# A linear-attention kernel: weight loads alternate, folds run in quarters, outputs and preparations move between slots

## The chip, the cores and the metric

The kernel runs on one core of one Trainium2 chip. The metric is the device time of one execution in microseconds (us), and the figure quoted for a kernel is the median of its runs. A run counts as slow when it is over 1.5% above the fastest of its kernel; unless the text says otherwise the runs below are all fast, and ratios use fast runs alone. A profile is one such execution under the hardware profiler; its span is 1.75 to 1.96 us shorter than the time of the same run (runs of e1 to e12 and of the kernel before beside them), so spans are compared with spans and times with times.

Engines: PE multiplies matrices, PEld loads PE's weights, DVE is the vector engine, ACT the scalar engine, POOL is GpSimd, SP issues the stores.

## The reference

```python
# q, k, v: [8 batches, 8 heads, 576, 64] float32; w_in [512, 2048], w_out [2048, 512]
q_p, k_p = phi(q), phi(k)                 # relu(.) times cos and sin of the position: 128 features
kv  = einsum('bhsf,bhsd->bhfd', k_p, v)
z   = sum(k_p, axis=2)
x   = (q_p @ kv) / (q_p @ z + 1e-6)       # then tokens x 512: x is [4608, 512]
out = softplus(x @ w_in) @ w_out          # [4608, 512] float32
```

The kernel does not run the second half as written. Near zero softplus(h) is close to h/2 + ln 2, so it folds the two weights once into `W_c` = 0.5 · w_in · w_out and a bias, and one product per tile is left. It keeps the squared norm of every row of x and of the weights; at the end it counts the rows whose norm lies under a limit, and where one is over, a general path computes everything again. That path is not taken here.

## The kernel before

The 4608 tokens are 36 tiles of 128. One pass of the main loop is called a slot; slot i attends tile i, transposes tile i-1, multiplies out tile i-4 and turns the queries of tile i+2.

```python
for i in range(4, NT):
    attend(i)                    # PE: numerators, denominators; DVE: rden (reciprocal), x
    if i > 4:
        transpose(i - 1)         # PE; move() is ACT's copy out of PSUM
        ...
    if i + 1 in first[2:]:
        keys(first.index(i + 1)) # PE: kv of the batch whose first tile is next
    if i != 6:
        emit(i - 3 if i < 6 else i - 4)   # PE: x @ W_c; DVE: + bias -> o_sb; SP: store
    if i + 2 < NT:
        turn(i + 2)              # PE: queries of tile i+2, out of POOL's reordered copy q_r
    if i > 4:
        norm(i - 1)              # on ACT, or on DVE for the tiles in NORMS_DVE
    for f, args in todo.get(i, []):
        f(*args)                 # preparation of later batches
```

The first tiles of the batches are `first = [0, 4, 9, 13, 18, 22, 27, 31]`. What the argument turns on is how a batch is prepared while an earlier one is attended. It takes four steps, in four slots one after the other:

```python
def prepare(b, n):
    if b < 4:
        ...                                   # batches 2 and 3: mostly on DVE
    else:
        if n < 3:
            relu_k(b) if n == 2 else values(b, 0, 2 * n)     # DVE
        values_pool(b, n, None if n == 3 else before)        # POOL: product n of four
        if n > 1:
            order_q(b, n - 2, POOL)                          # POOL: one half of q_r
    if n == (2 if b < 4 else 3) and b + 3 < B:
        ...                                   # POOL issues the loads of batch b + 3
...
at((4 if b == 2 else 8 if b == 3 else first[b] - 7) + n, prepare, b, n)
```

`before` is the newest addition of a bias on DVE: POOL's product (all but the fourth of a batch) waits until it is done, because DVE and POOL slow each other: in the profile before, a POOL product that starts 0.16 us behind one of DVE (58.43 against 58.27) takes 1.71 us, against 1.26 at best, and in e10 below a DVE norm that starts 0.08 us behind a POOL product takes 1.74 us, against 0.68 at best; e3 and e9 below measure it too. The program keeps POOL's work in the order in which it is written, so in steps 2 and 3 it does product, copy, product, copy, and the second copy is the last thing that the turning of the batch's first tile, in slot first[b]-2, needs.

The tail of the program:

```python
transpose(last); move(last // 2, 1, 2); norm(last)
emit(last - 3, "num"); emit(last - 2, "xT")
DVE.tensor_scalar(under, xn2, limit, 0.0, ALU.is_le, ALU.add, accum_out=count)
emit(last - 1)
PE.matmul(total, count, ones[:, 0:1], start=True, stop=True)
DVE.tensor_copy(flag, total)
emit(last, "num")
```

Of the kernel before, what the change touches and what calls it, by code (L numbers as in the profile page):

```python
# [12 lines left out]
F32 = mybir.dt.float32  # L13
# [35 lines left out]
def kernel(  # L49
# [16 lines left out]
    FB = 4  # L66
    C = 130
    LOADS, OUTS = 15, 16
    FT = D_FF // FB // 128
    NORMS_DVE = (13, 18, 22, 26, 28, 30, 32)  # L70
    AHEAD = [("q", 5), ("v", 6), ("k", 6), ("q", 6), ("v", 7), ("k", 7)]

    PE, DVE, SCL, POOL, SP = (
# [46 lines left out]
        POOL.iota(idx_i[64 * r : 64 * r + 64], pattern=[[1, T]], base=0, channel_multiplier=T)  # L120
    ident = singles.tile([128, 128], BF16)
    make_identity(nc, ident)
    load_w_in(0)
    for fb in range(FB):
        if fb + 1 < FB:
            load_w_in(fb + 1)
        load_w_out(fb)


# [162 lines left out]
    def attend(i):  # L292
        num = num_ps.tile([128, 4, 256], F32, tag="num", name="num_ps")
        (b0, t0), (b1, t1) = tiles[i]
        parts = [(b0, 0, 128)] if b0 == b1 else [(b0, 0, 64), (b1, 64, 64)]
        for hq in range(2):
            PE.matmul(
                ap(num[:, 2 * hq, 64:65], [(256, 2), (65, 2)]), ones_bf, eps_hi_lo,
                start=True, stop=True, skip_group_check=True,
            )  # L300
            for h2 in range(2):
                for b, p0, n in parts:
                    for c in range(2):
                        PE.matmul(
                            num[p0 : p0 + n, 2 * hq + h2, :C],
                            qTs[i][:, hq, c, h2, p0 : p0 + n],
                            blk_bufs[b % 3][:, h2, 2 * hq + c, :],
                            start=False, stop=True, skip_group_check=True,
                        )
        rden = small.tile([128, 4, 2], F32, tag="rden", name="rden")  # L310
        DVE.reciprocal(rden, ap(num[:, :, 64], [(256, 4), (65, 2)]))
        x = outs.tile([128, 4, 2, D], BF16, tag="x", name="x", bufs=3)
        DVE.tensor_mul(
            x, ap(num, [(256, 4), (65, 2), (1, D)]), ap(rden, [(2, 4), (1, 2), (0, D)])
        )
        xs[i] = x
# [38 lines left out]
    def store(i, o_sb):  # L355
        held.append((i, o_sb))
        while held and AHEAD[min(held[0][0], len(AHEAD) - 1)] in landing:
            i, o_sb = held.pop(0)
            ins = SP.dma_start(rows_of(i), o_sb)
            if i < len(AHEAD):  # L360
                tc.add_manual_dep(
                    ins.ins, landing[AHEAD[i]].ins.name,
                    mybir.DependencyInfo(mybir.DependencyClass.Sync, mybir.DependencyReason.DATA),
                    reason="the first stores leave the DMA engines to the loads",
                )

    def emit(i, place="out"):
        pool = {"out": out_ps, "xT": xT_ps, "num": num_ps, "turn": turn_ps}[place]
        nonlocal before
        ps = pool.tile([128, D_MODEL], F32, tag=place, name="o_ps")  # L370
        for g in range(4):
            PE.matmul(ps, xT_all[:, i, g, :], W_c[:, g, :], start=(g == 0), stop=(g == 3))
        o_sb = outs.tile([128, D_MODEL], F32, tag="o_sb", name="o_sb")
        before = DVE.tensor_add(o_sb, ps, b_bc)
        store(i, o_sb)


    wTs = {}
# [26 lines left out]
            col = FT * fb + ft  # L405
            SCL.activation(junk, wTs[fb][:, ft], ACT.Square, accum_out=wn2[:, col : col + 1])

    def fold(fb, r):
        if fb == 0:
            pool, tag = ((num_ps, "num"), (turn_ps, "turn"))[r]  # L410
            acc[r] = pool.tile([128, 2, 512], F32, tag=tag, name="wc_ps")
        ps = acc[r]
        for j in range(2):
            g = 2 * r + j
            for ft in range(FT):
                PE.matmul(
                    ps[:, j], wTs[fb][:, ft, g * 128 : g * 128 + 128], raw["w_out", fb][:, ft, :],
                    start=(fb == 0 and ft == 0), stop=(fb == FB - 1 and ft == FT - 1),
                )
        if fb == FB - 1:  # L420
            SCL.mul(
                W_c[:, 2 * r : 2 * r + 2].rearrange("p j m -> p (j m)"),
                ps.rearrange("p j m -> p (j m)"), 0.5,
            )
# [8 lines left out]
    def bias():  # L433
        ps = xT_ps.tile([128, D_MODEL], F32, tag="xT", name="b_ps")
        for ft in range(FT):
            PE.matmul(ps, ones_bf, raw["w_out", FB - 1][:, ft], start=(ft == 0), stop=False)
        yield
        PE.matmul(ps, ones, bsum, start=False, stop=True)
        SCL.mul(b_bc, ps, LN2)

# [41 lines left out]
    transpose(1)  # L482
    move(0)
    norm(0)
    turn_weights(1, 0)
    attend(3)
    transpose(2)
    sum_rows(0, POOL)
    for name in ("v", "k", "q"):
        load(name, 1)  # L490
    fold(0, 0)
    turn_weights(1, 1)
    transpose(3)
    move(1)
    norm(1)
    fold(0, 1)
    sum_rows(1, POOL)
    load("v", 2)
    load("k", 2)
    turn_weights(2, 0)  # L500
    norm(2)
    norm(3)
    weight_norms(0)
    fold(1, 0)
    turn_weights(2, 1)
    fold(1, 1)
    load("q", 2)
    load("v", 3)
    weight_norms(1)
    turn_weights(3, 0)  # L510
    sum_rows(2, DVE)
    fold(2, 0)
    turn_weights(3, 1)
    fold(2, 1)
    weight_norms(2)
    weight_norms(3)
    load("k", 3)
    load("q", 3)
    for n in range(4):
        values(1, n // 2, 2 * (n % 2))  # L520
    relu_k(1)
    for r in range(2):
        fold(3, r)
    parts = bias()
    next(parts)
    keys(1)
    next(parts, None)
    load("v", 4)
    load("k", 4)
    load("q", 4)  # L530
    for hq in range(2):
        order_q(1, hq, DVE)
    turn(4)
    emit(0)
    turn(5)

    todo = {}
# [4 lines left out]
    def prepare(b, n):  # L542

        if b < 4:
            if n == 3:
                relu_k(b)
            else:
                done = values(b, n // 2, 2 * (n % 2))
            if b == 2 and n == 2:
                values(b, 1, 2)  # L550
            if b == 3 and n < 2:
                values_pool(b, 2 + n, before)
            if n < 2 if b == 2 else n in (1, 2):
                order_q(b, n if b == 2 else n - 1, POOL, behind=done)
# [9 lines left out]

    for b in range(2, B):
        for n in range(4):
            at((4 if b == 2 else 8 if b == 3 else first[b] - 7) + n, prepare, b, n)
    parts = weight_limit()
    for i in (32, 34, 35):
        at(i, lambda: next(parts, None))  # L570
    for i in range(4, NT):
        attend(i)
        if i > 4:
# [4 lines left out]
                move((i - 1) // 2)  # L578
        if i + 1 in first[2:]:
            keys(first.index(i + 1))  # L580
        if i != 6:
            emit(i - 3 if i < 6 else i - 4)
        if i + 2 < NT:
            turn(i + 2)
        if i > 4:
            norm(i - 1)
        for f, args in todo.get(i, []):
            f(*args)
    tc.mark_branch_hint_location("guard", engines=[nc.tensor.engine, nc.scalar.engine, nc.sync.engine])
    last = NT - 1  # L590
    transpose(last)
    move(last // 2, 1, 2)
    norm(last)
    emit(last - 3, "num")
    emit(last - 2, "xT")


    under = small.tile([128, NT], F32, tag="under", name="under", bufs=1)
    count = small.tile([128, 1], F32, tag="count", name="count", bufs=1)
    DVE.tensor_scalar(under, xn2, limit, 0.0, ALU.is_le, ALU.add, accum_out=count)  # L600
    total = turn_ps.tile([1, 1], F32, tag="turn", name="total_ps")
    emit(last - 1)
    PE.matmul(total, count, ones[:, 0:1], start=True, stop=True)
    DVE.tensor_copy(flag, total)
    emit(last, "num")
    main.close()

    seen = nc.values_load(
# [81 lines left out]
```

## Time and profile before

| | before |
|---|---|
| time, median of 4 runs (lowest to highest) | 135.94 us (135.88 to 136.17) |
| profiled span | 134.5 us |
| busy: PE, DVE, ACT, POOL | 85%, 70%, 75%, 54% |
| DVE starts the reciprocal of slot 9, 25, 35 | 58.93, 98.23, 121.52 us |
| end of the last addition | 128.47 us |

The start of DVE's reciprocal in each slot is the time mark that I use to compare kernels: it is the first thing that follows the attending of a tile, there are 36 of them, and their differences say in which slot time was lost. The profiled execution took 136.39 us, 0.45 above that median, so a difference of spans against this profile overstates a gain by up to that much; where times and spans differ, the times decide. The page's lines on the engines, the slices, the DMA engines and the tail stand in the prediction.

### The profile page before, as it was taken

The page shows a single profiled execution, that of the slowest core. Times are in us where ns is not written, and L with a number is a line of the kernel's source. Part 1 is how long each engine was busy: PE and PEld are TensorE (multiplying, and loading weights), DVE is VectorE, ACT ScalarE, POOL GpSimd, SP SyncE. Part 2 cuts the span into 40 slices and gives each one's busy share as a digit, 9 for nine tenths or more (in the row PEclk, how much of TensorE's full clock was granted, in tenths as well). Part 3 has the DMA queues.
Part 4 walks back from the last instruction along what each step waited for, and adds up shares of the span by engine and source line. Part 5 has one row for each costly group of instructions (what it writes and reads, how often), then busy time and mean ns, then how long its engine had stood idle before and what let it go on. Part 6 is the DMA issues. An engine that isn't in the chain of part 4 may idle for free.

```text
span 134.5 us, 3821 instructions
## 1 busy us (share of the span) xinstructions
PE 114.4 (85%) x1539; PEld 76.9 (57%) x1558; DVE 94.6 (70%) x200; ACT 100.5 (75%) x188; POOL 72.1 (54%) x77
## 2 busy tenths in 40 slices
PE   0199998897988997999899999999999999998900
PEld 0035784454434575776667777776867776765300
DVE  5284593426593499789999968869997985995620
ACT  3399772999865659889889789889889888885200
POOL 6974106999623207757988998447975900000000
PEclk9999999999999999999999999999999999999997
DMA  1999999999999999999999999999999992342450
GB/s 8 178 207 208 207 203 205 206 207 208 208 208 208 207 207 208 208 208 211 205 208 207 208 208 246 236 240 239 288 395 390 357 355 96 121 160 79 176 219 7
DMA packets 22101, 28.07 MB, mean 209 GB/s; under 512 B 1088, under 2 KB 17472, under 8 KB 22080
## 3 DMA queue, kind: packets, MB, share of 16 engines
q0 software_dynamic: 16896, 18.35, 80.8%
q1 hardware_dynamic: 5184, 9.44, 18.9%
q8 instruction: 13, 0.21, 0.6%
q14 instruction: 8, 0.07, 0.2%
HBM read 36.70 MB, written 9.44 MB: 343 GB/s over the span
## 4 chain that ended last, share of the span: by engine, by line
PE 41%; DMA 22%; DVE 19%; POOL 7%; issue 4%; ACT 3%; DVEq 0%; POOLq 0%
PE o_ps L38 16%; DMA w_out_sb<-in_moe_w_out_dram 11%; DMA k_sb<-in_k_dram 11%; PE num_ps L38 8%; PE qT_ps L38 7%; DVE o_sb L38 6%; PE kv_ps L38 6%; DVE vcs L38 4%; DVE x L38 4%; PE xT_ps L38 4%; POOL bsum L38 3%; DVE k_sb L38 2%; POOL v_sb L38 1%; POOL w_in_sb L38 1%; DVE rden L38 1%
## 5 line engine op out<-in xcount | busy, mean ns | idle before, releaser
L38 ACT ACTIVATE qT<-qT_ps 128x1024 bf16<-128x1024 f32 (+1 forms) x37 | 36.9, 1002 | 12.0 <-PE qT_ps L38 11.3
L38 PE MATMUL o_ps<-W_c,xT_all 128*128 128x512 bf16 x129 | 35.2, 379 | 1.1 <-issue 0.3
L38 POOL TENSOR_TENSOR vcs<-v_sb,cs_tab 128x576 bf16<-128x576 bf16 x18 | 29.6, 1644 | 10.5 <-DVE o_sb L38 8.1
L38 DVE TENSOR_TENSOR o_sb<-o_ps,b_bc 128x512 f32<-128x512 f32 x36 | 24.7, 686 | 10.0 <-PE o_ps L38 9.6
L38 DVE TENSOR_TENSOR x<-num_ps,rden 128x512 bf16<-128x512 f32 x36 | 24.9, 692 | 3.1 <-ACT junk L38 0.4
L38 PE MATMUL num_ps<-kvblk,qT 128*128 128x130 bf16 (+1 forms) x320 | 24.3, 221 | 0.3 <-ACT qT L38 0.2
L38 PE MATMUL qT_ps<-diag,q_r 128*128 128x256 bf16 x144 | 22.1, 273 | 1.2 <-ACT qT L38 0.6
L38 ACT COPY xT_all<-xT_ps 128x1024 bf16<-128x1024 bf16 (+1 forms) x19 | 18.3, 961 | 4.2 <-PE xT_ps L38 4.2
L38 PEld LDWEIGHTS <-q_r 128*128 128x128 bf16 x144 | 13.5, 98 | 11.7 <-DVE q_r L38 2.1
L38 DVE TENSOR_TENSOR vcs<-v_sb,cs_tab 128x1152 bf16<-128x1152 bf16 x23 | 18.6, 833 | 1.5 <-DMA v_sb<-in_v_dram 1.5
L38 PEld LDWEIGHTS <-qT 128*128 128x128 bf16 (+1 forms) x320 | 17.5, 99 | 1.4 <-ACT qT L38 0.6
L38 PEld LDWEIGHTS <-xT_all 128*128 128x128 bf16 x144 | 12.5, 98 | 9.9 <-issue 0.2
L38 ACT ACTIVATE junk<-x 128x512 bf16<-128x512 bf16 x29 | 18.2, 627 | 0.0
L38 PE MATMUL wc_ps<-w_out_sb,wT 128*128 128x512 bf16 x61 | 14.5, 379 | 1.7 <-DMA w_out_sb<-in_moe_w_out_dram 1.5
L38 PEld LDWEIGHTS <-ones_bf 128*128 128x128 bf16 x94 | 9.5, 102 | 11.0 <-issue 7.6
L38 PE MATMUL xT_ps<-order,x 128*128 128x128 bf16 x144 | 13.9, 219 | 1.4 <-ACT xT_all L38 0.6
L38 PE MATMUL num_ps<-eps_hi_lo,ones_bf 128*128 128x4 bf16 x72 | 12.2, 169 | 0.0
L38 POOL COPY q_r<-q_sb 128x576 int32<-128x576 int32 x12 | 8.9, 746 | 5.3 <-DVE x L38 4.6
L38 ACT CAST kvblk<-kv_ps 64x520 bf16<-64x520 f32 x16 | 9.5, 593 | 2.6 <-PE kv_ps L38 2.5
L38 PE MATMUL busy_ps<-cs_tab,ones_bf 128*128 128x512 bf16 x17 | 5.8, 494 | 6.4 <-ACT cs_tab L38 6.3
L38 PEld LDWEIGHTS <-x 128*128 128x128 bf16 x144 | 9.7, 97 | 2.5 <-issue 2.1
L38 PE MATMUL kv_ps<-vcs,k_sb 64*64 64x130 bf16 x576 | 10.0, 218 | 1.1 <-DVE k_sb L38 1.0
(62 smaller groups left out, 127.5 us busy)
## 6 DMA issues: line engine op xcount, KB each, us to landing
out_dram<-o_sb SPq DMA_DIRECT2D x36, 256.0 KB, 4.4
v_sb<-in_v_dram POOLq DMA_DIRECT2D x8, 576.0 KB, 15.3
k_sb<-in_k_dram POOLq DMA_DIRECT2D x8, 576.0 KB, 18.1
q_sb<-in_q_dram POOLq DMA_DIRECT2D x8, 576.0 KB, 21.3
w_in_sb<-in_moe_w_in_dram POOLq DMA_DIRECT2D x4, 512.0 KB, 15.0
w_out_sb<-in_moe_w_out_dram POOLq DMA_DIRECT2D x4, 512.0 KB, 19.8
```

What stands on the lines that cost most here:

```text
L38: return self.tc.keep_in_program_order(f(*args, **kwargs))
```

## The change

Its intent is to use time in which PE waits for loads in the first third, and to empty the tail. The weights w_in and w_out are loaded in turn and folded in quarters between the turnings; all outputs of batch 0 come ahead of slot 4; POOL takes over a part of the value products of batches 1 and 2; the preparations of batches 4 to 7 start one slot later; three more norms go from ACT to DVE; the limit of the norms moves from slots 32, 34 and 35 to slots 10, 12 and 17; the epsilon products come first in `attend`; and the last output is multiplied out, added and stored in two halves. The diff, cut to its core:

```diff
-    NORMS_DVE = (13, 18, 22, 26, 28, 30, 32)
+    NORMS_DVE = (4, 6, 14, 18, 19, 23, 27, 28, 30, 32)
+    HALVES = (28, 29, 30)                      # these are stored in two halves
...
-    load_w_in(0)
     for fb in range(FB):
-        if fb + 1 < FB:
-            load_w_in(fb + 1)
+        load_w_in(fb)
         load_w_out(fb)
...
-    for n in range(4):
-        values(1, n // 2, 2 * (n % 2))
+    values(1, 0, 0)
+    values_pool(1, 2, None)
+    values(1, 0, 2)
+    values_pool(1, 3, None)
+    values(1, 1, 0)
     relu_k(1)
-    for r in range(2):
-        fold(3, r)
-    ...                                        # halves of bias() around keys(1)
+    for g in range(4):
+        fold(3, g)
+    bias()
+    emit(0)
+    emit(1, "num")
     keys(1)
     ...
+    emit(2, "xT")
     turn(4)
-    emit(0)
+    emit(3)
     turn(5)
...
-            if b == 2 and n == 2:
-                values(b, 1, 2)
-            if b == 3 and n < 2:
+            if n < 2:
                 values_pool(b, 2 + n, before)
...
-            at((4 if b == 2 else 8 if b == 3 else first[b] - 7) + n, prepare, b, n)
+            at((4 if b == 2 else 8 if b == 3 else first[b] - 6) + n, prepare, b, n)
     parts = weight_limit()
-    for i in (32, 34, 35):
-        at(i, lambda: next(parts, None))
+    at(10, next, parts)                        # the two others behind keys() in slots 12 and 17
...
-        if i != 6:
-            emit(i - 3 if i < 6 else i - 4)
+        if i > 7:
+            emit(i - 4)
...
+    norm(last)
+    emit(last - 3, "xT")
     transpose(last)
     move(last // 2, 1, 2)
-    norm(last)
-    emit(last - 3, "num")
-    emit(last - 2, "xT")
...
-    emit(last, "num")
+    emit_half(last, 0, "num")
+    emit_half(last, 1, "turn")
```

More of the change, by code (lines that the diff above doesn't have):

```diff
@@ L300, in attend @@
             )
+        for hq in range(2):
             for h2 in range(2):
@@ L358, in store @@
             i, o_sb = held.pop(0)
-            ins = SP.dma_start(rows_of(i), o_sb)
+            for a, z in ((0, 256), (256, 512)) if i in HALVES else ((0, 512),):
+                ins = SP.dma_start(rows_of(i)[..., a:z], o_sb[:, a:z])
             if i < len(AHEAD):
@@ L375, in emit, with emit_half @@
         store(i, o_sb)
+    def emit_half(i, half, place):
+        pool = {"num": num_ps, "turn": turn_ps}[place]
+        cols = slice(256 * half, 256 * half + 256)
+        ps = pool.tile([128, 256], F32, tag=place, name="o_ps")
+        for g in range(4):
+            PE.matmul(ps, xT_all[:, i, g, :], W_c[:, g, cols], start=(g == 0), stop=(g == 3))
+        o_sb = outs.tile([128, 256], F32, tag="o_sb", name="o_sb")
+        DVE.tensor_add(o_sb, ps, b_bc[:, cols])
+        SP.dma_start(rows_of(i)[..., cols], o_sb)
     wTs = {}
@@ L406, in weight_norms, with fold @@
             SCL.activation(junk, wTs[fb][:, ft], ACT.Square, accum_out=wn2[:, col : col + 1])
-    def fold(fb, r):
-        if fb == 0:
+    def fold(fb, g):
+        r, j = g // 2, g % 2
+        if fb == 0 and j == 0:
             pool, tag = ((num_ps, "num"), (turn_ps, "turn"))[r]
@@ L412, in fold @@
         ps = acc[r]
-        for j in range(2):
-            g = 2 * r + j
-            for ft in range(FT):
-                PE.matmul(
-                    ps[:, j], wTs[fb][:, ft, g * 128 : g * 128 + 128], raw["w_out", fb][:, ft, :],
-                    start=(fb == 0 and ft == 0), stop=(fb == FB - 1 and ft == FT - 1),
-                )
-        if fb == FB - 1:
+        for ft in range(FT):
+            PE.matmul(
+                ps[:, j], wTs[fb][:, ft, g * 128 : g * 128 + 128], raw["w_out", fb][:, ft, :],
+                start=(fb == 0 and ft == 0), stop=(fb == FB - 1 and ft == FT - 1),
+            )
+        if fb == FB - 1 and j:
             SCL.mul(
@@ L436, in bias @@
             PE.matmul(ps, ones_bf, raw["w_out", FB - 1][:, ft], start=(ft == 0), stop=False)
-        yield
         PE.matmul(ps, ones, bsum, start=False, stop=True)
@@ L484 @@
     norm(0)
-    turn_weights(1, 0)
     attend(3)
@@ L491 @@
     fold(0, 0)
-    turn_weights(1, 1)
+    fold(0, 1)
+    turn_weights(1, 0)
     transpose(3)
@@ L495 @@
     norm(1)
-    fold(0, 1)
+    fold(0, 2)
+    turn_weights(1, 1)
+    fold(0, 3)
     sum_rows(1, POOL)
@@ L499 @@
     load("k", 2)
-    turn_weights(2, 0)
     norm(2)
@@ L504 @@
     fold(1, 0)
+    turn_weights(2, 0)
+    fold(1, 1)
     turn_weights(2, 1)
-    fold(1, 1)
+    fold(1, 2)
+    fold(1, 3)
     load("q", 2)
-    load("v", 3)
-    weight_norms(1)
-    turn_weights(3, 0)
-    sum_rows(2, DVE)
-    fold(2, 0)
-    turn_weights(3, 1)
-    fold(2, 1)
+    weight_norms(1)
+    fold(2, 0)
+    fold(2, 1)
+    turn_weights(3, 0)
+    sum_rows(2, DVE, 0, 1)
+    fold(2, 2)
+    turn_weights(3, 1)
+    fold(2, 3)
+    sum_rows(2, DVE, 1)
+    load("v", 3)
     weight_norms(2)
@@ L518 @@
     load("q", 3)
-    for n in range(4):
-        values(1, n // 2, 2 * (n % 2))
-    relu_k(1)
-    for r in range(2):
-        fold(3, r)
-    parts = bias()
-    next(parts)
+    values(1, 0, 0)
[3 more added lines that the diff above has]
+    values(1, 1, 0)
+    relu_k(1)
+    for g in range(4):
+        fold(3, g)
+    bias()
+    emit(0)
+    emit(1, "num")
     keys(1)
-    next(parts, None)
     load("v", 4)
@@ L580 @@
             keys(first.index(i + 1))
-        if i != 6:
-            emit(i - 3 if i < 6 else i - 4)
+            if i in (12, 17):
+                next(parts, None)
+        if i > 7:
+            emit(i - 4)
         if i + 2 < NT:
             turn(i + 2)
-        if i > 4:
+        if 4 < i:
             norm(i - 1)
@@ L600 @@
     DVE.tensor_scalar(under, xn2, limit, 0.0, ALU.is_le, ALU.add, accum_out=count)
-    total = turn_ps.tile([1, 1], F32, tag="turn", name="total_ps")
+    emit(last - 2, "num")
     emit(last - 1)
+    total = xT_ps.tile([1, 1], F32, tag="xT", name="total_ps")
     PE.matmul(total, count, ones[:, 0:1], start=True, stop=True)
     DVE.tensor_copy(flag, total)
-    emit(last, "num")
+    emit_half(last, 0, "num")
+    emit_half(last, 1, "turn")
     main.close()
```

## The prediction

> **What bounds the kernel now.** Times inside the kernel are microseconds of the profiled span (134.5 us; the timed runs give 135.94). A "slot" is one pass of the main loop: one tile of 128 tokens is attended, an earlier one is transposed, and the output of the tile four slots back is multiplied out. I read the page's slices first.
>
> ```profile
> PE 114.4 (85%) x1539; PEld 76.9 (57%) x1558; DVE 94.6 (70%) x200; ACT 100.5 (75%) x188; POOL 72.1 (54%) x77
> PE   0199998897988997999899999999999999998900
> DMA  1999999999999999999999999999999992342450
> GB/s 8 178 207 208 207 203 205 206 207 208 208 208 208 207 207 208 208 208 211 205 208 207 208 208 246 236 240 239 288 395 390 357 355 96 121 160 79 176 219 7
> ```
>
> Two things are full at once. The DMA engines are full from slice 2 to slice 32, so the moment at which any load lands is set by the bytes ahead of it. PE is nearly full from slice 20 on, and is the bound of the second half. By the issues of single loads plus their times to landing, wo3 (the last weight) lands at 34.1, v1 37.0, k1 39.8, q1 42.6, q2 51.2, q5 76.9, k7 94.4, q7 98.7: 2.85 us for each 576 KB until stores join.
>
> The stretches then read so. Up to 41 the chain of waits runs through loads. From 45 to 68 it alternates between DVE and keys; from 68 to 90 and from 98 on it is PE. In steady state the PE timeline shows 2.05 us a slot (attend at 112.4, 114.4, 116.45), made of turn 0.44, attend 0.51, transpose 0.22, output 0.86. With keys (1.2) that is about 9.4 us for four slots. The DVE-bound stretches cost little over that: slots 9 to 12 last from 57.9 to 68.4, 10.5 us against 9.4, and the later ones lose 0.2 to 0.35 each: about 2 us in all.
>
> Next, what pins the middle. The first six stores wait for named loads, and there are 16 output buffers, so the addition for output 20 needs the store of output 4 to have landed, and that for 21 the store of 5. The output tile's rows for the issue near 90.8, then the DVE and PE timeline near 97:
>
> ```profile
> L38 SPq DMA_DIRECT2D out_dram<-o_sb x1: 539/539/539, 90.8 to 90.8; - x1
> ...
> DMA to landing us min/median/max: 6.0/6.0/6.0
> ```
>
> ```profile
> 96.95 0.69 DVE L38 TENSOR_TENSOR o_sb<-o_ps,b_bc 128x512 f32<-128x512 f32 x1
> 97.69 1.02 PE L38 MATMUL o_ps<-W_c,xT_all 128*128 128x512 bf16 x4
> 99.44 0.69 DVE L38 TENSOR_TENSOR o_sb<-o_ps,b_bc 128x512 f32<-128x512 f32 x1 [0.29 <-DMA out_dram<-o_sb]
> ```
>
> Store 4 lands at 90.8 + 6.0 = 96.8, and addition 20 starts at 96.95. PE's product 21 uses the single output bank that this addition empties (97.64) and starts at 97.69. So slot 25 is already within 0.1 us of a date set by the DMA stream. Nothing gained before it can be kept.
>
> Last, the tail, where the limit of the norms sits in PE's path:
>
> ```profile
> 120.16 0.38 PE L38 MATMUL row_ps<-ident,wm 128*1 128x128 f32 x2
> ...
> 123.31 0.16 DVE L38 RECIPROCAL rec<-col_ps 128x1 f32<-128x1 f32 x1
> ...
> 123.52 0.38 PE L38 MATMUL xT_ps<-order,x 128*128 128x128 bf16 x4 [0.55 <-DVE rec L38]
> ...
> 127.78 0.69 DVE L38 TENSOR_TENSOR o_sb<-o_ps,b_bc 128x512 f32<-128x512 f32 x1 [0.50 <-PE o_ps L38]
> ```
>
> [...] The 256 KB stores of the quiet tail land 2.4 us after issue[...]. [...] POOL's products here take 1.26 us at best and 1.67 in the median, its q copies 0.66 alone and 1.15 beside VectorE's products. [...]
>
> **The change part by part.**
>
> *Weights alternate, folds in quarters.* The bytes are the same, so k1 and q1 land when they did. wo2 moves from seventh to sixth, so from 31.6 to about 28.8, and wi3 takes 31.6. What PE still owes after wi3 is two turnings (0.61 each), two quarter folds (0.85 each) and fold 3 [...]: it ends near 38 instead of 39.1. The gain of 1.1 us fills a wait for k1, so by itself it moves nothing.
>
> *Outputs 0 to 3 before slot 4.* Three outputs of 0.86 us leave slots 4, 5 and 7. The bias product (0.86 + 1.13) now comes whole before outputs 0 and 1, so PE runs 38.0 bias, 40.0 outputs 0 and 1, 41.7 keys of batch 1 (before: 40.65), 42.9 output 2, 43.75 turn 4 (43.19), and attends tile 4 near 45.75 (45.5). Slots 4 to 7 then run at the pace of the one turning bank, turn 0.44 plus ACT's 1.02 plus hand-over, some 1.65 us instead of 1.9, so PE could turn tile 9 by 52. But that needs q2, landed at 51.2, and POOL's two q copies:
>
> ```profile
> 51.39 2.31 POOL L38 COPY q_r<-q_sb 128x576 int32<-128x576 int32 x2 [4.60 <-DVE x L38]
> ...
> 53.76 0.39 PE L38 MATMUL qT_ps<-diag,q_r 128*128 128x256 bf16 x2 [0.16 <-POOL q_r L38]
> ```
>
> The built order has POOL do product, copy, product, copy for batch 2; before it was copy, copy. The second product (1.3 to 1.7) therefore stands between the copies: 51.4 + 0.7 + 1.6 + 0.7 = 54.4 or somewhat more, against 53.7. Attend 8, keys 2 and slot 9 follow in PE's order. Slot 9 starts about 0.7 us later than before, not earlier.
>
> *Slots 9 to 25.* The work in a slot is unchanged (output i-4). Preparations start one slot later, which takes a DVE product of up to 1.84 us out of slot 11, ahead of keys 3 (worth 0.3 to 0.5). One more norm is on DVE in this stretch, ACT having slack. The row and column products of the limit come into slots 12 and 17 at about 0.3 us each. Sum at slot 25: +0.7 - 0.4 + 0.6 - 0.5 (smoother DVE, guessed as a quarter of its 2 us) = +0.4 us, and it cannot be below -0.1 by the pin.
>
> *Epsilon products first.* The same 72 products and as many weight loads. In the PE timeline one costs about 0.03 us before its numerators start. Nothing either way.
>
> *Slots 33 to 35 and the tail.* Row and column leave: slot 34, which has no turn, takes 2.05 us now and should take 1.6 (-0.45). From attend 35 (120.54), the last addition ends 7.93 us later at 128.47. Afterwards, counting from attend 35: attend 0.93, transpose 0.33, outputs 31 and 32 to 2.98, transpose 35 to 3.2, outputs 33 and 34 to 4.9, the count 0.2, two half outputs of 0.43 to 5.96. The flag and two half additions [...] end near 6.65. That is -1.3 us, of which a second store issue (0.54 us each) on the queue may take 0.1 to 0.2 back: -1.2. [...]
>
> Sum: +0.4 - 0.45 - 1.2 = -1.25, thus about 134.7; since the DVE relief may be larger than I guess, I put it at 134.5.
>
> **Rivals.** (1) *The front gains and keeps it*: 2.6 us of PE work leaves slots 4 to 7 and all later slots move forward, 131 to 133. For it speaks a chain that is PE for 41% of the span; against it the landing of q2 at 51.2 and the store pin at slot 25. (2) *The pin is reached exactly*: POOL's product does not hurt and DVE is smoother, so slot 25 stands where it did and only the tail counts: 135.94 - 0.1 - 1.65 = 134.2. (3) *The front slips by 1.5 us or more*, because keys of batch 1 wait for POOL's two products or POOL runs slower beside VectorE; the tail gain is eaten: 135.8 to 136.3. For it speaks that POOL now stands in the path of both keys 1 and turn 9, and that each POOL load waits for the eighth load before it (its issues at 37.6, 40.4, 43.2 follow landings at 37.0, 39.8, 42.6).
>
> **Range and chances.** The ceiling on the gain is about 0.1 + 0.45 + 1.4 = 1.95 us, to 134.0; 2% would be 2.7. I allow for an error of 0.3 in the pin, hence 133.7 at the low end and 135.9 at the high one. Faster by over 2%: 0.07, if I misread the pin. Slower by over 2%: 0.02. Within: 0.91.
>
> **What would show it.** Slot 9's attend near 58.6 (57.9 before); turn 9's second half after a POOL product; addition 20 at or after 96.8; no row or column product after 85; the last addition 6.5 to 6.8 us after attend 35. If the attend of slot 26 came before 98, the pin would be wrong; if slot 9 came before 57, the POOL step would be.

## The result, and the profile after

The changed kernel takes 140.78 us (140.72 to 140.92, four runs). Its ratio to the kernel before is 1.035, with a 95% interval from 1.034 to 1.037: slower, and well outside the predicted range. A ratio here is the mean time of one kernel's fast runs over the mean of the other's in the same rounds, so it is not quite the ratio of the two medians.

From the page of the changed kernel, the span, the busy time of each engine, PE's busy tenths in 40 slices, and the engines of the chain that ended last:

```profile
span 138.9 us, 3838 instructions
...
PE 114.2 (82%) x1544; PEld 77.3 (56%) x1562; DVE 98.4 (71%) x205; ACT 98.5 (71%) x182; POOL 77.3 (56%) x81
...
PE   0199989999996776899899699789979987999910
...
PE 16%; POOL 7%; ACT 5%; DVE 2%; issue 1%; DMA 1%; DVEq 0%; POOLq 0%; ACTq 0%
```

PE has the same work (114.2 us against 114.4) in a span that is 4.4 us longer. Slices 5 to 11 are better filled than before, as intended; slices 12 to 15 (41.7 to 55.6 us), which the early outputs have left, are emptier. The second half, where PE was at 9 almost throughout, now has dips in slices 22, 25, 29 and 32 to 33 (counted from 0, 3.47 us each), and POOL is the second engine of the chain. (The view could follow this chain back only to 88.41 us, so its shares add up to a third of the span.) The list of waits over the whole execution says what PE waits for (the columns are total time, how often, and the longest):

```profile
PEld L38 <- POOL q_r L38: 6.7, 6, 1.5
...
PE qT_ps L38 <- POOL q_r L38: 5.1, 5, 1.2
```

The second line is PE's matmuls of `turn`, waiting for POOL's reordered queries. Before, that line read 0.2 us, one wait. One of the five lies in the front; the other four, together 4.4 us, end at 79.30, 90.75, 103.86 and 115.35: once in each of batches 4, 5, 6 and 7. (The line for PEld is the same waits seen by the weight loads, and is not added.)

The time marks by slot give the same places:

| reciprocal of slot | before | after | later by |
|---|---|---|---|
| 4 | 46.21 | 48.09 | 1.88 |
| 9 | 58.93 | 60.09 | 1.16 |
| 16 | 76.38 | 77.44 | 1.06 |
| 18 | 81.75 | 84.40 | 2.65 |
| 22 | 91.41 | 95.33 | 3.92 |
| 25 | 98.23 | 102.00 | 3.77 |
| 27 | 103.77 | 108.66 | 4.89 |
| 31 | 113.07 | 119.61 | 6.54 |
| 34 | 119.44 | 125.99 | 6.55 |
| 35 | 121.52 | 127.50 | 5.98 |
| end of the last addition | 128.47 | 133.03 | 4.56 |

The front costs 1.2 us, four steps between slots 16 and 31 cost 5.5 us, and the tail gives 2 us back.

One of the steps close up, batch 5. The lines are from the timeline (start, duration, engine, operation, out<-in with shapes, how many, and in brackets the idle time before it and what ended it). First the kernel before:

```profile
81.32 1.66 POOL L38 TENSOR_TENSOR vcs<-v_sb,cs_tab 128x576 bf16<-128x576 bf16 x1 [0.39 <-DVE o_sb L38]
...
82.92 0.66 POOL L38 COPY q_r<-q_sb 128x576 int32<-128x576 int32 x1
83.54 1.27 POOL L38 TENSOR_TENSOR vcs<-v_sb,cs_tab 128x576 bf16<-128x576 bf16 x1
...
84.76 0.66 POOL L38 COPY q_r<-q_sb 128x576 int32<-128x576 int32 x1
...
86.62 0.60 PE L38 MATMUL qT_ps<-diag,q_r 128*128 128x256 bf16 x4
```

And the changed kernel:

```profile
86.14 1.66 POOL L38 TENSOR_TENSOR vcs<-v_sb,cs_tab 128x576 bf16<-128x576 bf16 x1 [0.52 <-DVE o_sb L38]
...
87.75 0.66 POOL L38 COPY q_r<-q_sb 128x576 int32<-128x576 int32 x1
88.37 1.72 POOL L38 TENSOR_TENSOR vcs<-v_sb,cs_tab 128x576 bf16<-128x576 bf16 x1
89.27 0.38 PE L38 MATMUL qT_ps<-diag,q_r 128*128 128x256 bf16 x2
90.03 0.65 POOL L38 COPY q_r<-q_sb 128x576 int32<-128x576 int32 x1
90.75 0.39 PE L38 MATMUL qT_ps<-diag,q_r 128*128 128x256 bf16 x2 [1.09 <-POOL q_r L38]
```

Both are the same four POOL instructions, released by DVE's addition. Before, they end at 85.42 and PE turns the batch's first tile at 86.62: 1.2 us of slack. After, the addition that releases them is that of the next slot, so relative to PE everything comes about 2 us later; PE does the first half of the turning at 89.27, finds the second copy missing, and stands for 1.09 us. The slack of the other batches before was of the same kind: the copies ended at 75.84, 97.70 and 107.87, the turnings began at 76.54, 98.55 and 108.57, so 0.7, 0.85 and 0.7 us.

### The profile page after: what moved, and what is told of

It is laid out like the page before. It is cut to its first block, busy times and chain, and to the rows that moved or that the text cites. A ratio compares the mean times of both kernels' runs of the same rounds, so it can differ in the third digit from the quotient of the medians.

```text
span 138.9 us, 3838 instructions
## 1 busy us (share of the span) xinstructions
PE 114.2 (82%) x1544; PEld 77.3 (56%) x1562; DVE 98.4 (71%) x205; ACT 98.5 (71%) x182; POOL 77.3 (56%) x81
## 5 line engine op out<-in xcount | busy, mean ns | idle before, releaser
L38 POOL TENSOR_TENSOR vcs<-v_sb,cs_tab 128x576 bf16<-128x576 bf16 x22 | 35.2, 1602 | 16.6 <-DVE o_sb L38 12.4
L38 PE MATMUL o_ps<-W_c,xT_all 128*128 128x512 bf16 (+1 forms) x134 | 35.5, 373 | 0.9 <-issue 0.3
L38 DVE TENSOR_TENSOR o_sb<-o_ps,b_bc 128x512 f32<-128x512 f32 (+1 forms) x37 | 24.7, 671 | 9.2 <-PE o_ps L38 8.8
L38 PE MATMUL num_ps<-kvblk,qT 128*128 128x130 bf16 (+1 forms) x320 | 22.8, 220 | 0.8 <-ACT qT L38 0.6
L38 DVE TENSOR_TENSOR vcs<-v_sb,cs_tab 128x1152 bf16<-128x1152 bf16 x21 | 19.8, 961 | 0.2 <-DMA v_sb<-in_v_dram 0.2
L38 PEld LDWEIGHTS <-qT 128*128 128x128 bf16 (+1 forms) x320 | 17.0, 99 | 1.3 <-ACT qT L38 1.0
L38 ACT ACTIVATE junk<-x 128x512 bf16<-128x512 bf16 x26 | 16.3, 627 | 0.0
L38 PE MATMUL busy_ps<-cs_tab,ones_bf 128*128 128x512 bf16 x17 | 6.7, 557 | 6.4 <-ACT cs_tab L38 6.3
L38 DVE COPY wT<-wT_ps 128x512 bf16<-128x512 bf16 x16 | 6.0, 418 | 7.5 <-PE wT_ps L38 4.2
L38 DVE RECIPROCAL rden<-num_ps 128x8 f32<-128x8 f32 x36 | 7.3, 202 | 5.7 <-PE num_ps L38 5.6
```

Source lines behind the costliest of these rows:

```text
L38: return self.tc.keep_in_program_order(f(*args, **kwargs))
```

## The experiments

My theory after the comparison: (A) the later preparations put POOL's last copy into PE's path, and this is most of the loss; (B) the front adds about 1 us; (C) the tail's gain is real. The rivals: that the loss comes with the new table of norms (POOL is late because DVE is), or with the front, which arrives at the middle in a bad rhythm. All twelve kernels gave correct results, and the compared runs are all of the fast state. They were run in four sets on four chips; the kernel before, run again beside each set, took 135.96 to 136.06 us in the median, so medians of different sets are compared below.

### e1: the changed kernel, preparations as before

```diff
-            at((4 if b == 2 else 8 if b == 3 else first[b] - 6) + n, prepare, b, n)
+            at((4 if b == 2 else 8 if b == 3 else first[b] - 7) + n, prepare, b, n)
```

> The changed kernel with one number put back: batches 4 to 7 are prepared from slot first-7 on, not first-6. Theory A (the later preparation makes POOL's second q copy late for the turning of each batch's first tile, 1.1 to 1.2 us in each of four batches): 135.6 to 136.6 us, and PE's waits for POOL's q copies fall from 5.1 us to under 1. Theory B (the late start of slot 4, caused by POOL's products for batch 1, is the root, and the later waits follow from it): still 139.5 or more. Theory C (more norms on DVE, or the epsilon order): still above 140.

Measured: 137.88 us, ratio 1.013 (1.010 to 1.015). The one figure takes back 2.9 of the 4.8 us, but not all; the forecast of theory A for the time (135.6 to 136.6) is missed, that for the waits is met. Of PE's waits for POOL's copies after 55 us, 0.8 us is left, at 55.03 in the front. In their place PE waits for DVE's x (PE 1.9 us in two waits, PEld 2.8 us in three). The timeline near slot 16, the first of three slots (16, 21 and 25) that each lose 1.7 to 2.0 us against e5 below, part of which is made up again:

```profile
76.99 0.81 POOL L38 DMA_DIRECT2D v_sb<-in_v_dram  x1
...
77.61 1.82 DVE L38 TENSOR_TENSOR vcs<-v_sb,cs_tab 128x1152 bf16<-128x1152 bf16 x1
...
79.66 0.69 DVE L38 TENSOR_TENSOR x<-num_ps,rden 128x512 bf16<-128x512 f32 x1
80.41 0.40 PE L38 MATMUL xT_ps<-order,x 128*128 128x128 bf16 x4 [0.96 <-DVE x L38]
```

DVE's value product takes 1.82 us, which is 0.75 when nothing is in its way; POOL issues three loads from 76.99 to 79.29. x comes late behind it, and PE's transpose waits 0.96 us. The new table has put a DVE norm just ahead of that product (0.68 us from 77.00); in e5 below, which has none there, the product starts at 76.70, ahead of the issuing, and takes 0.92. In the other two slots a norm stands ahead again, but POOL is not issuing loads: DVE's value product (from 90.93 and from 101.04) starts 0.39 and 0.51 us behind a product of POOL and takes 1.83 and 1.82 us. That the issuing holds DVE's product up is not shown: in the kernel before, a product among three issues (65.63, issues from 64.21 to 66.76) also takes 1.84 us, but one that starts during an issue at 77.81 takes 0.75, and so does one at 78.83 in e2, within POOL's issues. So the two parts of the change belong together: with only one taken back, the other does harm. What e1 leaves open is how much the table does on its own.

### e2: the kernel before, preparations one slot later

```diff
-            at((4 if b == 2 else 8 if b == 3 else first[b] - 7) + n, prepare, b, n)
+            at((4 if b == 2 else 8 if b == 3 else first[b] - 6) + n, prepare, b, n)
```

> The kernel before with only that number changed (first-6 in place of first-7). Theory A: 139.5 to 141 us, with PE waiting for POOL's q copies some 4 to 5 us in all. Theory B and C: within 0.7 us of 135.94.

Measured: 141.73 us, ratio 1.042 (1.039 to 1.045). This one figure alone makes the old kernel slower than the whole change does, and slower than I forecast. The kind of waits is not wholly mine, though. Between 58 and 120 us:

```profile
PE xT_ps L38 <- DVE x L38: 3.2, 3, 1.1
...
PE qT_ps L38 <- POOL q_r L38: 1.1, 1, 1.1
```

PE waits 1.1 us for POOL's copy and 3.2 us for x of DVE. With the old table of norms, DVE's x is late more often than POOL's copy. At 98.45, for instance, DVE's relu starts 0.37 us behind a product of POOL and takes 1.83 us instead of 0.75, and the reciprocal of slot 24 stands behind it. The table of norms thus decides which of the two engines comes late; the shift costs PE its time either way.

### e5 and e6: the preparations and the table of norms together

```diff
 # e5, from the changed kernel
-    NORMS_DVE = (4, 6, 14, 18, 19, 23, 27, 28, 30, 32)
+    NORMS_DVE = (13, 18, 22, 26, 28, 30, 32)
-            at((4 if b == 2 else 8 if b == 3 else first[b] - 6) + n, prepare, b, n)
+            at((4 if b == 2 else 8 if b == 3 else first[b] - 7) + n, prepare, b, n)
 # e6, from the kernel before: the same two edits, the other way
```

> The changed kernel with the preparation back at first-7 and the tuple of norms on DVE back to that of before. With the first of these alone PE still waited 3 us or so for x from DVE at slots 16, 21 and 25[...]. Theory A2 (start of the preparation and choice of norms belong together; both together cost what the middle lost): 135.2 to 136.3 us, no wait for x near 1 us left. Rival (the front's 1.2 us and POOL's product in batch 2 go on costing in each batch): 137 or more.

> The kernel before with first-6 and the changed kernel's tuple of norms: the later preparation without the mismatch of norms. Theory A: PE waits for POOL's q copies 4 to 5 us in all and the time is 139 to 140.5, less than the 141.7 of first-6 with the old tuple. Rival (the mismatch was all of that run's loss, POOL's lateness none): 136 to 137.

Measured: e5 135.27 us, ratio 0.996 (0.993 to 1.000). e6 142.07 us, ratio 1.046 (1.042 to 1.050). In the waits of e6 between 58 and 122:

```profile
PE qT_ps L38 <- POOL q_r L38: 4.1, 4, 1.1
```

These are waits of the same number and size as in the changed kernel (4.4 us, 4 times), in a kernel that has nothing of the front or the tail. (The forecast of the waits is met; that of the time, 139 to 140.5 and less than e2, is not.) So these two lines of the diff are enough for the whole slowdown, and without them the rest of the change gains 0.7 us. The combinations, in us; "rest" is everything else in the change:

| | preparations at first-7 | at first-6 |
|---|---|---|
| old norms, old rest | 135.94 | 141.73 |
| new norms, old rest | not run | 142.07 |
| old norms, new rest | 135.27 | not run |
| new norms, new rest | 137.88 | 140.78 |

At first-6 the kernel is slow with either table. The table alone costs 2.6 us in the new rest at first-7, and little at first-6, where it exchanges waits for x for waits for POOL.

### e8: the changed kernel, POOL's copy ahead of its last product

This leaves the shift as it is and only exchanges POOL's order for batches 4 to 7, so that the second half of the queries does not stand behind the fourth product.

```diff
+            if n == 3:
+                order_q(b, 1, POOL)
             values_pool(b, n, None if n == 3 else before)
-            if n > 1:
-                order_q(b, n - 2, POOL)
+            if n == 2:
+                order_q(b, 0, POOL)
```

> The changed kernel, only POOL's order turned for batches 4 to 7: the second q copy ahead of the fourth value product. Theory A (PE waits because a product of 1.7 us stands before the second copy): the waits of PE for POOL's q copies in slots 15 to 30 fall from 4.4 us to under 0.8 us, the time to 135.5 to 137.3. Rival (POOL is short of throughput, so the wait moves to keys, which need the product): 139 or more, with PE waiting for POOL's products before keys.

Measured: 137.16, 135.57, 137.10 and 137.18 us, median 137.13, ratio 1.005 (0.999 to 1.012). The same batch 5 as above, timeline of e8:

```profile
86.06 1.65 POOL L38 TENSOR_TENSOR vcs<-v_sb,cs_tab 128x576 bf16<-128x576 bf16 x1 [2.28 <-DVE o_sb L38]
...
87.66 1.73 POOL L38 COPY q_r<-q_sb 128x576 int32<-128x576 int32 x2
...
89.01 0.84 PE L38 MATMUL qT_ps<-diag,q_r 128*128 128x256 bf16 x4
89.36 1.27 POOL L38 TENSOR_TENSOR vcs<-v_sb,cs_tab 128x576 bf16<-128x576 bf16 x1
```

Both copies come before the fourth product, and PE's four turning matmuls run in one piece, 0.84 us instead of 0.60 and no 1.09 us of standing. The waits of PE's matmuls for q_r between 58 and 122 fall from 4.4 us to none that the list shows (the weight loads still wait 1.1 us in all), and the median falls by 3.65 us, by nothing but the order of two POOL instructions. This shows that in the changed kernel the late copy is the cause of most of the loss, not merely a symptom of late DVE work. Something is left: in slot 18 the first of the four gains is lost again. It still starts at 84.33 (84.40 in the changed kernel), because DVE's next value product meets two POOL products in a row and takes 2.16 us, and the reciprocal stands behind it:

```profile
82.25 2.16 DVE L38 TENSOR_TENSOR vcs<-v_sb,cs_tab 128x1152 bf16<-128x1152 bf16 x1
```

Why one of the four runs is 1.5 us faster is not shown: the profile is of a run at 137.16.

### e3: batch 1 prepared by DVE alone

```diff
-    values(1, 0, 0)
-    values_pool(1, 2, None)
-    values(1, 0, 2)
-    values_pool(1, 3, None)
-    values(1, 1, 0)
+    for n in range(4):
+        values(1, n // 2, 2 * (n % 2))
```

The reason for it, in the timeline of the front. Before, DVE makes the four products of batch 1 and then relu of its keys:

```profile
37.02 2.76 DVE L38 TENSOR_TENSOR vcs<-v_sb,cs_tab 128x1152 bf16<-128x1152 bf16 x4 [1.47 <-DMA v_sb<-in_v_dram]
39.84 0.76 DVE L38 TENSOR_SCALAR k_sb<-k_sb 128x2304 bf16<-128x2304 bf16 x1
```

In the changed kernel DVE makes three and POOL the rest, as two smaller ones, at the same time:

```profile
37.36 5.10 DVE L38 TENSOR_TENSOR vcs<-v_sb,cs_tab 128x1152 bf16<-128x1152 bf16 x3 [0.21 <-DMA v_sb<-in_v_dram]
38.65 2.51 POOL L38 TENSOR_TENSOR vcs<-v_sb,cs_tab 128x576 bf16<-128x576 bf16 x2
...
43.19 1.24 PE L38 MATMUL kv_ps<-vcs,k_sb 64*64 64x130 bf16 x72 [1.11 <-DVE k_sb L38]
```

Three products take 5.10 us where four took 2.76, the keys of batch 1 start at 43.19 instead of 40.65, and PE waits for them. Taking a product away from DVE has made DVE slower by 2.3 us, because POOL's help is in its way: in e3, which is without it, the keys start at 41.91.

> The changed kernel with batch 1's four value products all on DVE again. Theory A with the front's delay passed on to the end (preparations are started by slots): keys of batch 1 start near 41.7 instead of 43.2, and the time is 139.3 to 140.2. Rival: the later waits are tied to landings and swallow the front's 1.2 us: 140.5 to 141. Theory B: 137 or less.

Measured: 141.63 us, ratio 1.040 (1.037 to 1.044). That is a miss for me. Slot 4 is early as it should be, 46.82 against 48.09, and slot 7 still (52.69 against 54.31 in the changed kernel), but slot 9 comes at 61.33, 1.2 us later than in the changed kernel. PE is held up by POOL's second copy of batch 2, as in the changed kernel, and then runs slowly. The first two lines are of this run's timeline, the next two of the changed kernel's, and the last two are from this run's page, where PEclk is the clock granted to PE in each of the 40 slices, in tenths of full speed:

```profile
55.02 0.39 PE L38 MATMUL qT_ps<-diag,q_r 128*128 128x256 bf16 x2 [2.01 <-POOL q_r L38]
56.34 2.16 PE L38 MATMUL kv_ps<-vcs,k_sb 64*64 64x130 bf16 x72
```

```profile
54.97 0.39 PE L38 MATMUL qT_ps<-diag,q_r 128*128 128x256 bf16 x2 [0.68 <-POOL q_r L38]
56.56 1.24 PE L38 MATMUL kv_ps<-vcs,k_sb 64*64 64x130 bf16 x72 [0.26 <-DVE k_sb L38]
```

```profile
PE   0199989999999673999899699969979997999920
PEclk9999999999999999599999999999999999999997
```

PE comes earlier and waits 2.01 instead of 0.68 us, but the copy ends at the same time in both kernels (the turning goes on at 55.02 and 54.97), so this wait takes the lead away and no more. POOL's first copy waits in both for q of batch 2 to land (it starts at 51.49 and 51.65), which is what the prediction had put in the way of the front. What makes slot 9 later than in the changed kernel is the rate of PE: its keys take 2.16 instead of 1.24 us and the output behind them 1.19 instead of 0.81 (together 1.3 us), and TensorE's granted clock was 0.50 from 57 to 59 us, where the changed kernel had 1.00. The drop follows the wait in the trace; that the wait caused it is not shown. All four runs of e3 have a lower mean clock (0.977 to 0.981) than those of the changed kernel (0.985 to 0.992). So the cause in the front is right (slot 4; the keys of batch 1 start at 41.91, where I said 41.7), the lead ends at POOL's copy for batch 2, and the time of this run cannot be used to say what the front is worth.

### e7: both batches 1 and 2 prepared as before

```diff
 # from e5
-    values(1, 0, 0) ... values(1, 1, 0)        # the five lines above
+    for n in range(4):
+        values(1, n // 2, 2 * (n % 2))
-            if n < 2:
+            if b == 2 and n == 2:
+                values(b, 1, 2)
+            if b == 3 and n < 2:
                 values_pool(b, 2 + n, before)
```

> The changed kernel with the preparation and norms of before, and batches 1 and 2 prepared as before too; what is left of the change is the alternating weights, quarter folds, outputs 0 to 3 ahead of slot 4, epsilon order, and the tail. The prediction's argument (q2's landing and the store pin at slot 25 leave the front nothing to gain): within 0.5 us of the kernel before with the tail alone (135.3), so 134.8 to 135.8. Rival (moving outputs forward is worth its 2.6 us of PE work): 133.5 or less.

Measured: 135.50 us, ratio 0.998 (0.994 to 1.003), inside the forecast of the prediction's argument. What is left of the change here is the order of loads, the folds, the early outputs and the tail. Slot 8 starts at 54.96 (55.79 in e5, so POOL's share of batches 1 and 2 costs 0.8 us there), and slot 25 at 98.82. Compare e4 below, which has the old front: 99.01. So the front of the change, which takes 2.6 us of PE work out of slots 4 to 7, is worth 0.2 us by slot 25. That lead is then lost: between slots 27 and 28 this kernel takes 3.54 us against 2.30 in e5. The profiles of e9 and e10 below, one of each, show most of the reason.

### e4: the kernel before with the new tail

```diff
-    for i in (32, 34, 35):
-        at(i, lambda: next(parts, None))
+    at(10, next, parts)
...
             keys(first.index(i + 1))
+            if i in (12, 17):
+                next(parts, None)
...                                             # and the tail of the change, with emit_half
```

> The kernel before with only the tail of the change: the limit of the norms in slots 10, 12 and 17, the last slots reordered, the last output in halves. By the prediction's sum: 0.45 us from slot 34 and 1.2 from the tail, less up to 0.6 for the products that go to slots 12 and 17: 134.2 to 134.9 us. Rival: the end is set by the last transfer and its completion, which do not move: 135.7 or more.

Measured: 135.31 us, ratio 0.995 (0.991 to 0.998): it gains some 0.7 us, between the two forecasts. In its profile slot 18 starts at 82.52, 0.77 us later than before, since the row and column products of the limit now stand in slots where PE is full. The span is 133.4, 1.1 us shorter (0.7 by the times): so the end gains about 1.5 to 1.9 us and the middle takes 0.8 of it. In the changed kernel the end of the timeline reads:

```profile
131.51 0.69 DVE L38 TENSOR_TENSOR o_sb<-o_ps,b_bc 128x512 f32<-128x512 f32 x1 [0.17 <-PE o_ps L38]
132.19 0.85 DVE L38 TENSOR_TENSOR o_sb<-o_ps,b_bc 128x256 f32<-128x256 f32 x2
```

It ends at 133.03, 6.4 us after the first product of attend 35 (126.61); before that was 128.47 and 120.47, 8.0 us.

### e9, e10 and e11: the limit still earlier, and the pin of the stores

e4 suggests putting the limit's two products where PE has room. e9 puts them into slots 4 and 6; slot 6 has no output.

```diff
 # e9, from e4
-    at(10, next, parts)
+    at(4, next, parts)
+    at(6, next, parts, None)
-        if i != 6:
+        if i == 6:
+            next(parts)
+        else:
             emit(i - 3 if i < 6 else i - 4)
-        row = turn_ps.tile([1, 128], F32, tag="turn", name="row_ps")   # and col, too
+        row = out_ps.tile([1, 128], F32, tag="out", name="row_ps")
 # e10, from e9
-    LOADS, OUTS = 15, 16
+    LOADS, OUTS = 15, 17
 # e11, from e9
-    emit_half(last, 0, "num")
-    emit_half(last, 1, "turn")
+    emit(last, "num")
```

> The kernel before with the changed tail, but the limit of the norms worked out in slots 4 and 6, where the output bank is free and PE waits for ACT and DVE, not in slots 12 and 17, where PE is full (the tail alone with slots 12 and 17 arrived 0.7 us later at slot 18). Theory: slot 18 stands again within 0.2 us of where it stood before, slot 34 is 0.45 us shorter, the end after attend 35 is 1.4 us shorter: 134.1 to 134.8 us, about 0.6 below the run with the tail alone. Rival (the tail's gain is lost in the last transfers whatever precedes): 135.2 or more.

> The same with 17 output buffers in place of 16, which moves every wait for an early store by one slot. If the store pin at slot 25 that the prediction rests on still binds: 0.1 to 0.4 us faster than with 16, and no wait of an output addition for a store. If it does not bind: within 0.1 us.

> The early-limit kernel with its last output whole again, not in halves. The halves let the last addition take some 0.42 us, not 0.69, after PE's last product, and put a 128 KB store last: whole should be 0.2 to 0.5 us slower. Rival (a second store issue eats it): within 0.1 us or faster.

Measured, six runs each: e9 134.15 to 137.23 us, median 135.66; two of the runs (137.23 and 136.87) count as slow, and the ratio of the four fast ones is 0.996 (0.993 to 0.999). e10 136.38 (135.84 to 136.71), ratio 1.003 (1.001 to 1.005). e11 135.59 (134.64 to 137.07, one of them slow), ratio 0.997 (0.993 to 1.001). The four fast runs of e9 alone spread over 1.7 us; the six of e12 below spread over 0.2. Nothing can be said from these of halves against a whole last output; that question is inconclusive. Slot 18 of e9 starts at 81.93, 0.18 us later than in the kernel before, so moving the limit did what was forecast there; the median is not in the forecast range. For e10 both forecasts failed: it is not faster than e9, and additions still wait for stores. The profile of e9 is that of its fastest run.

They do show two other things. The first is the pin of the prediction. Until the last output e9 and e11 are the same program, and slot 24 starts at 96.06 and 96.10. In e9 the store of output 4 landed at 96.5; in e11 at 98.0, and there addition 20 waited for it:

```profile
98.11 0.69 DVE L38 TENSOR_TENSOR o_sb<-o_ps,b_bc 128x512 f32<-128x512 f32 x1 [1.02 <-DMA out_dram<-o_sb]
```

Slot 25 then starts at 99.38 instead of 98.40. So the pin is there, but its date is not fixed: a store's landing moves by more than 1 us. The store of output 4, of 256 KB, took 5.9 to 7.6 us from issue to landing in e9, e11 and e10, which are nearly the same program; the 36 stores of the kernel before took 2.4 to 7.1. A seventeenth buffer (e10) removes this wait, addition 20 starting at 97.16 although the store lands at 98.5, but there is a wait of this kind two additions later (1.00 us at 102.69), as there is with 16 buffers in e4 (1.00 us at 103.11) and e5 (0.79 us at 103.46). Its time is no better.

The second is what makes these kernels unsteady. In e10 slot 28 comes 3.55 us after slot 27, in e9 2.31 us. The timeline of e9 at that place:

```profile
105.29 0.86 DVE L38 SCALAR_TENSOR_TENSOR junk_v<-x 128x512 bf16<-128x512 bf16 x1
105.56 1.71 POOL L38 TENSOR_TENSOR vcs<-v_sb,cs_tab 128x576 bf16<-128x576 bf16 x1
```

And that of e10:

```profile
105.75 1.27 POOL L38 TENSOR_TENSOR vcs<-v_sb,cs_tab 128x576 bf16<-128x576 bf16 x1
105.83 1.74 DVE L38 SCALAR_TENSOR_TENSOR junk_v<-x 128x512 bf16<-128x512 bf16 x1
```

It is the same norm and the same product. In e9 DVE starts 0.27 us ahead: the norm takes 0.86 us and POOL's product pays with 1.71. In e10 POOL starts 0.08 us ahead: its product takes 1.27, and the norm, which stands in front of the next reciprocal, takes 1.74. So a shift of a third of a microsecond makes the norm 0.88 us longer. In one place of the changed kernel the earlier start did not spare DVE: a product that starts at 38.03, 0.62 us ahead of POOL's first product (38.65), takes 3.76 us and ends after POOL's second; why is open. (The remaining third of the 1.24 us by which the slots differ is an x that starts late after its reciprocal, by 0.67 us against 0.31; why is open.) e7 shows the second order too (product at 105.77, norm at 105.84 for 1.75 us), and that is where its lead went. That the spread of e9's fast runs is this same toss is argued only: one run of each kernel is profiled. The three slow runs of e9 and e11 have the lowest mean clocks of their set (0.977 to 0.980, the others 0.984 to 0.994), so for them the clock is a rival explanation.

### e12: the parts that help, together

```diff
 # from e5: the limit in slots 4, 5 and 6, in the output's bank
-    at(10, next, parts)
+    at(4, next, parts)
+    at(5, next, parts)
+    at(6, next, parts, None)
...
-            if i in (12, 17):
-                next(parts, None)
```

> The changed kernel with the preparation and the norms of before (135.27 us in its run) and the limit of the norms worked out in slots 4 to 6, where no output is multiplied out, in place of 10, 12 and 17. If the limit's products cost about 0.6 us in the full slots: 134.4 to 135.0 us and slot 18 about 0.6 us earlier than in that run. If stores' landings near slot 25 or clashes of DVE with POOL take it back: 135.0 to 136.5, with a spread of more than 1 us between runs, as in the last three.

Measured: 134.59 us (134.55 to 134.76, six runs), ratio 0.989 (0.988 to 0.991): 1.1% faster than the kernel before, a small gain but clear of the noise, and steady. From its page:

```profile
span 132.8 us, 3841 instructions
...
PE   0099989999998979789989999999999999999910
```

PE's second half is full again. Slot 18 starts at 82.53 (83.10 in e5): the 0.57 us that the limit's products no longer take from full slots reach the end almost whole (span 132.8 against 133.4).

## Why the prediction was wrong

It said 134.5 us, from 133.7 to 135.9; the result was 140.78.

**The step that failed** is the one under "Slots 9 to 25": "Preparations start one slot later, which takes a DVE product of up to 1.84 us out of slot 11, ahead of keys 3 (worth 0.3 to 0.5)." It booked the shift as a gain on DVE and did not ask when the shifted work must be done. POOL's product, copy, product and copy of a batch take about 4.5 us from the addition that releases them to the end (86.14 to 90.68 in the lines above); in the profile before they were done 0.7 to 1.2 us ahead of the turning that needs them; a slot is 2.05 us. The subtraction, made with numbers that were all in that profile, gives copies late by 0.9 to 1.4 us, four times. Measured were 1.24, 1.09, 0.89 and 1.15. The error is of sign, not of size: slot 25 was put at +0.4 us and came at +3.8, and two of the four waits come after slot 25. e6 and e8 show it from both sides. e2 shows that the gain was small where it was looked for (slot 13 comes 0.27 us earlier, measured from slot 11, and slot 15 is already 1.5 us late), and that with the old table of norms the same shift makes DVE late too (3.2 us of waits for x). The third rival did name POOL as the danger, but only in the front, and the chance given to a slowdown of over 2% was 0.02.

**Weights and folds**: the loads landed within 0.4 us of what was said (wo3 at 34.4, v1 at 37.3, k1 at 40.1), and PE is fuller there. The prediction put fold 3 at 3.4 us; the matmuls of the folds start 0.216 us apart in the profile before (33.79, 34.01, 34.22, 34.44), which makes 3.45 for its 16 and 0.86 for a quarter fold (0.85 was said). No run took weights and folds alone, so what they are worth is not shown.

**Outputs forward**: "Nothing gained before it can be kept" held: 0.2 us at slot 25 (e7 against e4). The reason given was too narrow. The store pin binds in e11, but in the changed kernel no addition waits for a store before 129 us: addition 20 comes at 100.61, long after. The gain is spent earlier: e7, which prepares batches 1 and 2 as before, is ahead of e4 by 0.23 us at slot 8 and 0.19 at slot 9.

**Keys of batch 1 and slot 9**: keys were expected at 41.7 and started at 43.19, though the products before them came nearly as said (bias at 38.46 for 38.0, outputs 0 and 1 at 40.18 for 40.0); DVE's three products, 5.10 us beside POOL's, are the mis-sized term, and without POOL (e3) keys start at 41.91. Slots 4 to 7 took 1.71 to 2.38 us each (before, 2.11 to 2.65; 1.65 was said) and made up a part, so slot 9 came 1.16 us later where 0.7 was said. The second POOL product between the copies of batch 2 did what was said: PE waited 0.7 us for that copy.

**One more norm on DVE** counted for nothing in the prediction. With the preparations at first-7 the new table costs 2.6 us (e1 against e5).

**The limit in slots 12 and 17**: put at 0.6 us; e4 is later by 0.77 at slot 18.

**Epsilon first**: nothing was expected; no run took it alone, and the attending took the same 0.51 us of PE in steady slots before and after.

**The tail**: right. Slot 34 took 1.5 to 1.6 us as said. The last addition ended 6.4 us after attend 35 where 6.5 to 6.8 was said, and two halves of the addition cost 0.85 us together, against 0.69 for a whole one; the prediction's sum took an estimate of the author's for them. (The halved stores of outputs 28 to 30 no run took alone. The last store, which SP issues, landed 4.0 us after its issue whole in the kernel before and 3.7 us as a half in the changed kernel, but 3.7 us whole in e11 too, so a saving by the half is not shown.) The 2 us are in the changed kernel, hidden under a loss of 6.5.

## What to carry to other kernels

When a change moves work to a later slot, look for its last consumer and subtract: the end of the work and the start of what needs it, both read from the profile before, against the length of a slot. Work on an engine off the critical path (POOL is busy 54% here) has a deadline all the same, and its slack is the number to look up, not its busy share. Two parts of a schedule that were tuned together, like the table of norms and the start of the preparations, have to be moved together, and an engine's help is no gain where both engines get in each other's way (here 5.10 us for three DVE products beside two of POOL's, 2.76 for four of DVE alone).
